# Chunked attention and a mixer on one core: batch 0's values, row sums and first products in another order

## The chip, the cores and the metric

The kernel runs on one core of a Trainium2 chip. TensorE (PE) multiplies matrices, VectorE (DVE), ScalarE (ACT) and GpSimd (POOL) work on elements, SyncE (SP) issues transfers. The metric is the device time of one execution in microseconds (us); less is better.

## What is computed

Four batches, 768 rows, 8 heads of 64 columns. Each chunk of 32 rows attends to the 16 rows before it, itself, the 8 rows behind it and 8 memory rows. What comes out, 512 columns wide, goes through a mixer.

```python
for c in range(S // 32):
    l, r = max(0, 32 * c - 16), min(S, 32 * c + 40)
    k_full = concat([mem_k, k[:, :, l:r]])
    v_full = concat([mem_v, v[:, :, l:r]])
    a = softmax(scale * q_c @ k_full.T)        # the sum gets 1e-9 added
    x[32 * c : 32 * c + 32] = a @ v_full
u = x + ((x.T @ U) @ V).T                      # U is 768 x 32, V is 32 x 768
out = u + relu(u @ w_ch1) @ w_ch2              # 512 x 2048, 2048 x 512
```

U, V and the weights arrive as 64-bit floats; the kernel reads them as pairs of 32-bit words and makes 32-bit numbers from each pair.

## The kernel before

The kernel begins with the attention of batch 0 (`attention(0, xs)`, from L516; its own script stands from L806 to L927). Only when that is done can the mixer of batch 0 (`both_blocks`) and then the other batches (`sevens`) run; their attention is woven into the mixer of the batch before.

Batch 0 goes in three parts of 256 rows (T = 0, 1, 2), each in two sides (s or g = 0, 1) and two tiles of 128 rows (t). A part passes through these steps:

- `load_k`, `load_q` (transfers), `regroup` (L567, copies that sort rows by parity: on VectorE, for part 2 on GpSimd), `k_part` and `q_part` (TensorE turns them, L618; ScalarE and VectorE copy them out of PSUM into `kall` and `qt`).
- `s_turn` (L698): TensorE's scores, 64 small products, 128 records in the trace. `s_weights` (L720, L721, L724): VectorE's maximum and difference, ScalarE's exponential, for each side a tile `pt`. `s_sums` (L729 to L734): VectorE's row sums and their reciprocals `rs`.
- `t_part` (L752): TensorE turns the weights, ScalarE copies them (L755).
- `av_part` (L772): the product with the values in `vbs[T]`, 64 small products; VectorE scales them by `rs` into `x` (L784).
- `collect` (L796): x.T @ U of one tile of 128 rows, into one PSUM bank that holds the sum over all six.

The values come in `load_v` (L600, L607), eight or ten transfers a part, onto a home that GpSimd has filled first with the memory's values, copied to eight blocks of 256 elements (`spread_mv`, L826). U and V are loaded by `load_consts` and made into floats by the class `Words`: `begin` is one ScalarE instruction for each raw tile (L230), then four on VectorE (L237, L245, L250, L257); `u3` is U's result written three times. `spread_v` (L282 to L288) puts V into the form in which it is multiplied. `stream` does the same to the mixer's weights, one step with each `advance(1)`.

When all is collected, `turn_x` (L1133) and `turn_x1` (L1157) turn x for the two blocks of the mixer, and `join_uT` (L1142) adds V's product. `keep_clock(n)` puts n products of a tile of zeros (`busy`, L143) in front of the next bank that TensorE takes.

The order of instructions is written out by hand for SyncE, TensorE, ScalarE, GpSimd and VectorE in this stage (`manual_schedule`): each engine runs its instructions in the order of the script between two `yield`s, with the pieces between `yield`s in order. Each engine waits in order, so an instruction that waits holds all behind it. The small tables at the top (`PROBS`, `GAP`, `LOADS`, `CHAIN`) choose which tiles hold the weights of a part, how many fillers stand where, and the order of the loads.

## Time and profile before

| what | value |
|---|---|
| time, median of 3 runs | 653.67 us (652.35 to 654.86) |
| profiled execution | span 652.5 us from first to last instruction; no time besides is given for it |
| TensorE matmuls busy | 628.0 us, 96% |
| VectorE, ScalarE, GpSimd busy | 367.2, 235.2, 80.9 us |
| attention of batch 0 | about the first 52 us |

A row of a timeline has a start, a duration (both us), the engine, the line, the operation, `out<-in` with shapes, and how often it was merged. In brackets at its end: how long the engine sat idle before it, and what released it. "issue" stands for a wait for nothing that the profile shows. TensorE executes a 32-bit product in two records where the program has one.

### The profile page before, as it was taken

The numbers are of one execution on the slowest core, as the hardware profiler recorded it, in microseconds if no ns is written. First come the engines' busy times: TensorE is split into PE (matmuls) and PEld (weight loads), VectorE is DVE, ScalarE is ACT, GpSimd is POOL, SyncE is SP. The second block draws the span as 40 slices with busy tenths as digits, with TensorE's granted clock in tenths as the row PEclk, the third lists the DMA queues.
The fourth block names the chain that finished last, engine by engine and source line by source line (L and its number), as shares of the span: only waits on it lengthen the run. The fifth ranks groups of instructions, "written<-read, shape, count | busy, mean of one in ns | idle before, by whom it ended". The sixth has DMA issues, their size and how long they took to land.

```text
span 652.5 us, 14945 instructions
## 1 busy us (share of the span) xinstructions
PE 628.0 (96%) x6075; PEld 543.8 (83%) x6078; DVE 367.2 (56%) x703; ACT 235.2 (36%) x557; POOL 80.9 (12%) x106
## 2 busy tenths in 40 slices
PE   8688999999899999999999998999999999999997
PEld 5557899998787888889888897899978899999886
DVE  6947788898784747745643835443445632222322
ACT  4525544447332545522213622321225412121221
POOL 5100000043054465100400000000000000000000
PEclk9989999999999999999999999999999999999999
DMA  9893667667888699676599669667422056555301
GB/s 241 156 354 140 201 221 240 216 204 169 183 183 227 166 314 272 192 187 171 137 258 198 136 178 296 181 179 186 130 70 92 1 172 182 147 162 160 99 2 48
DMA packets 168704, 115.02 MB, mean 176 GB/s; under 512 B 100956, under 2 KB 139484, under 8 KB 168636
## 3 DMA queue, kind: packets, MB, share of 16 engines
q1 hardware_dynamic: 168012, 113.92, 63.0%
q8 instruction: 48, 0.79, 0.5%
q10 hardware_dynamic: 624, 0.15, 0.1%
q14 instruction: 20, 0.16, 0.1%
HBM read 90.83 MB, written 28.97 MB: 184 GB/s over the span
## 4 chain that ended last, share of the span: by engine, by line
PE 61%; DMA 4%; DVE 4%; SPq 2%; issue 1%; ACT 1%; POOL 1%; ACTq 0%
PE ps_h L1301 24%; PE acc L1532 18%; PE acc L1542 9%; DMA blocks<-spread 2%; PE ps_a L772 2%; PE acc L1526 2%; PE ps_h L1481 2%; DMA w1l<-w1s 1%; PE ps_a L698 1%; PE ps_a L1197 1%; SPq L600 1%; PE ps_a L802 1%; PE ps_a L752 1%; DMA w1s<-sums 1%; DVE x L1497 1%
## 5 line engine op out<-in xcount | busy, mean ns | idle before, releaser
L1532 PE MATMUL acc<-w,hh 128*128 128x512 f32 x612 | 158.3, 394 | 0.0
L1532 PEld LDWEIGHTS acc<-w,hh 128*128 128x128 f32 x612 | 112.9, 188 | 19.8 <-issue 0.5
L1542 PE MATMUL acc<-w,hl 128*128 128x512 f32 x306 | 87.2, 393 | 0.0
L1542 PEld LDWEIGHTS acc<-w,hl 128*128 128x128 f32 x306 | 56.8, 188 | 11.9
L1301 PE MATMUL ps_h<-t12h,w1l 128*128 128x384 f32 x192 | 55.8, 344 | 0.6 <-ACT c L1327 0.6
L1301 PE MATMUL ps_h<-bh,w1l 128*128 128x384 f32 x192 | 52.9, 340 | 0.0
L1301 PE MATMUL ps_h<-t34h,w1l 128*128 128x384 f32 x152 | 46.6, 347 | 1.9 <-issue 1.5
L1481 PE MATMUL ps_h<-uh,w1h 128*128 128x384 f32 x124 | 42.5, 347 | 2.2 <-ACT w1h L387 1.2
L1481 PE MATMUL ps_h<-ul,w1h 128*128 128x384 f32 x124 | 41.3, 337 | 0.4 <-DVE ul L1179 0.4
L1316 DVE SCALAR_TENSOR_TENSOR hl<-ps_h,hh 128x384 fp32r<-128x384 f32 x29 | 16.1, 555 | 44.0 <-ACT hh L1315 43.9
L1323 DVE TENSOR_TENSOR c<-ps_h,c 128x384 f32<-128x384 f32 x19 | 10.5, 553 | 51.6 <-PE ps_h L1301 51.6
L1301 PEld LDWEIGHTS ps_h<-t12h,w1l 128*128 128x128 f32 x192 | 35.3, 188 | 3.2 <-ACT c L1327 1.0
L1315 ACT ACTIVATE hh<-hst 128x384 fp32r<-128x384 f32 x36 | 18.9, 526 | 49.9 <-PE acc L1532 44.7
L1316 DVE SCALAR_TENSOR_TENSOR hl<-hst,hh 128x384 fp32r<-128x384 f32 x36 | 20.0, 557 | 29.0 <-PE acc L1542 28.5
L1301 PE MATMUL ps_h<-b,w1l 128*128 128x384 f32 x174 | 35.4, 339 | 0.5 <-DVE hst L1323 0.5
L1301 PEld LDWEIGHTS ps_h<-bh,w1l 128*128 128x128 f32 x192 | 35.1, 188 | 0.8
L1323 DVE TENSOR_TENSOR hst<-ps_h,hst 128x384 f32<-128x384 f32 x36 | 20.0, 555 | 27.4 <-ACT hst L1327 18.0
L1315 ACT ACTIVATE hh<-ps_h 128x384 fp32r<-128x384 f32 x29 | 14.2, 491 | 51.6 <-PE ps_h L1301 51.4
L1301 PE MATMUL ps_h<-t12l,w1l 128*128 128x384 f32 x96 | 32.4, 337 | 0.0
L1301 PEld LDWEIGHTS ps_h<-t34h,w1l 128*128 128x128 f32 x152 | 27.9, 188 | 4.4 <-issue 2.9
L1301 PEld LDWEIGHTS ps_h<-b,w1l 128*128 128x128 f32 x174 | 30.9, 188 | 0.8 <-DVE hst L1323 0.8
L1327 ACT COPY c<-ps_h 128x384 f32<-128x384 f32 x19 | 9.1, 479 | 59.7 <-PE ps_h L1301 59.7
(250 smaller groups left out, 1208.1 us busy)
## 6 DMA issues: line engine op xcount, KB each, us to landing
w1l<-w1s SPq DMA_DIRECT2D x155, 256.0 KB
rw<-in_moe_w_ch_dram SPq DMA_DIRECT2D x14, 512.0 KB
out_dram<-x SPq DMA_DIRECT2D x24, 256.0 KB
blocks<-spread SPq DMA_DIRECT2D x24, 256.0 KB
vb<-in_v_dram SPq DMA_DIRECT2D x56, 98.0 KB
raw<-in_moe_w_ch_dram SPq DMA_DIRECT2D x20, 256.0 KB
rw<-in_moe_w_ch_dram SPq DMA_DIRECT2D x16, 256.0 KB
w1s<-sums SPq DMA_DIRECT2D x16, 256.0 KB
```

Source lines behind the costliest of these rows:

```text
L600: nc.sync.dma_start(out=vt[r0:r0 + NW - NM, n0:n1, D * j:D * j + D], in_=bass.AP(rows.tensor, rows.offset, [[step, count], [CK * step, n1 ...
L698: nc.tensor.matmul(out=psv[s][(slice(CK * i, CK * i + CK), t) + ((p // 2, p % 2) if b >= DIRECT else (p % 2, p // 2))], lhsT=qt[p // 2][ro ...
L772: nc.tensor.matmul(out=psv[g][CK * i:CK * i + CK, t, j], lhsT=pt[s][rows, 2 * t + k_, CK * i:CK * i + CK], rhs=vt[rows, NI * t + i, D * j: ...
L1301: nc.tensor.matmul(out=ps[:, :TOK], lhsT=w_, rhs=u, start=(start and m == 0), stop=(m == 5), skip_group_check=True,)
L1315: nc.scalar.activation(out=hh, in_=c, func=AF.Relu)
L1316: nc.vector.scalar_tensor_tensor(out=hl, in0=c, scalar=0.0, in1=hh.bitcast(F32), op0=ALU.max, op1=ALU.subtract,)
L1323: nc.vector.tensor_tensor(out=out, in0=ps[:, :TOK], in1=in1, op=ALU.add)
L1327: nc.scalar.copy(out=out, in_=ps[:, :TOK])
L1481: nc.tensor.matmul(out=ph[:, :TOK], lhsT=w[:, c, :], rhs=u[c], start=(m == 0), stop=(m + 1 == len(parts)),)
L1526: nc.tensor.matmul(out=acc[tt], lhsT=h[:, sl], rhs=w, start=False, stop=(m == 2))
L1532: nc.tensor.matmul(out=acc[tt], lhsT=h[:, sl], rhs=w, start=(begins and m == 0), stop=False,)
L1542: nc.tensor.matmul(out=acc[tt], lhsT=hl[:, sl], rhs=w2h[f], start=False, stop=ends is not None)
```

## The change

It touches the script of batch 0 alone.

- Loads: memory values, then k and q of part 0, then parts 1 and 2, U, the values of part 0, V, the values of parts 1 and 2, then the weights. V's three transfers thereby go behind the ten of the first values. GpSimd copies the memory's values to the second home right after the first, and to the third right after the memory keys.
- Row sums of parts 0 and 1: `fold` adds halves on GpSimd, six instructions for a side, into the tile `spare`; `invert` adds 1e-9 and takes the reciprocal on VectorE, just before the part's product. Part 2 keeps `s_sums`, behind the product of part 1.
- `t_part(0)` stands before the third scores instead of behind them.
- V's unpacking (`v_words`) stands behind the second weights and before the third ones, on VectorE and ScalarE. U's is one piece sooner.
- `av_part(2)` stands before the collects of tiles 2 and 3, not behind `turn_x`.
- Fillers: three before `av_part(1)`; none before `av_part(2)` and none behind the last collects.
- `PROBS`: the weights of part 1 lie in the tiles 7 and 8 of the second matrix and no longer in 0 and 1.

```diff
-PROBS = [5, 0, 9]
-GAP = [2, 2, 2]
-LOADS = 'mv t1 t2 uv v0 v1 v2 a0 b0 w1 w2'
-CHAIN = [8, 4]
+PROBS = [5, 7, 9]
+GAP = [2, 2, 3]
+LOADS = 'a0 b0 w1 w2'
...
+        def fold(T):
+            rs = rss[T] = sm.tile([P, 2, 2, 2, 2], F32, name="rs", bufs=3)
+            for s in range(2):
+                halves = spare.rearrange("n (s a w) -> n s a w", s=2, w=NW // 2)[:, s]
+                w, wide_ = NW // 2, pts[T, s].rearrange("n (a w) -> n a w", w=NW)
+                while w > 1:
+                    nc.gpsimd.tensor_tensor(
+                        out=halves[:, :, 0:w], in0=wide_[:, :, 0:w], in1=wide_[:, :, w:2 * w], op=ALU.add,
+                    )
+                    w, wide_ = w // 2, halves
+                two_ = halves.rearrange("n (t k g) w -> n t k g w", t=2, k=2)
+                nc.gpsimd.tensor_tensor(
+                    out=rs[:, :, :, :, s].rearrange("n t g k -> n t k g"),
+                    in0=two_[:, :, :, :, 0], in1=two_[:, :, :, :, 1], op=ALU.add,
+                )
+
+        def invert(T):
+            nc.vector.tensor_scalar_add(out=rss[T], in0=rss[T], scalar1=1e-9)
+            nc.vector.reciprocal(out=rss[T], in_=rss[T])
...
             mk = fetch_memk()
-            take(1)
-            take(1)
-            spread_mv(vbs[0])
-            take(2)
+            load(1)
+            load(2)
+            load_U()
+            for n in two:
+                spread_mv(vbs[n])
+                fill_v(n)
+                if n == 0:
+                    load_V()
...
             place_memk()
+            spread_mv(vbs[2])
+            fill_v(2)
+            for what, m in loading:
+                what(m)
             regroup(kraw, kn, "kn", 1)
...
             u_words.begin()
-            s_sums(0)
-            yield
-            keep_clock(GAP[1])
-            sc = s_turn(1)
-            for h in two:
-                q_part(2, h)
             u_words.shift()
             u_words.low()
...
+            yield
+            keep_clock(GAP[1])
+            sc = s_turn(1)
+            fold(0)
             nc.gpsimd.tensor_copy(out=u_sb, in_=u3[:, :, 0, :])
+            for h in two:
+                q_part(2, h)
+            for s in two:
+                t_part(0, s)
             s_weights(1, *sc)
+            v_words.begin()
+            v_words.shift()
+            v_words.low()
+            val = v_words.join()
             yield
             sc = s_turn(2)
-            for s in two:
-                t_part(0, s)
+            fold(1)
             s_weights(2, *sc)
-            v_words.begin()
-            s_sums(1)
+            invert(0)
             av_part(0)
             yield
             for s in two:
                 t_part(1, s)
-            s_sums(2)
-            v_words.shift()
-            v_words.low()
-            val = v_words.join()
+            keep_clock(GAP[2])
+            invert(1)
             av_part(1)
-            take(len(loading))
+            yield
             for s in two:
                 t_part(2, s)
+            s_sums(2)
             for t in two:
                 collect(t)
             spread_v(val)
             yield
             advance(1)
+            wide[0] = None
+            av_part(2)
             for t in two:
                 collect(2 + t)
             early = turn_x(range(NCK))
-            wide[0] = None
-            keep_clock(GAP[2])
             advance(4)
-            av_part(2)
             yield
             advance(1)
             for t in range(4, NT):
                 collect(t)
-            keep_clock(CHAIN[0])
             turned.extend(turn_x1(c) for c in range(3))
```

What that does to the order of instructions, at three places. On GpSimd, from the first copy of the memory's values (`vb_114`, `vb_115` and `vbe` are the homes of parts 0, 1 and 2), before:

```order
L826 COPY vb_114<-mv 128x2048
L626 COPY kall<-memkT 128x32x8 x2
L567 COPY kn<-kraw 128x4x2x64 x2
L826 COPY vb_115<-mv 128x2048
L567 COPY qn<-qraw 128x4x2x64 x2
L826 COPY vbe<-mv 128x2048
L626 COPY kall<-memkT 128x32x8
```

and in the change:

```order
L842 COPY vb_114<-mv 128x2048
L842 COPY vb_115<-mv 128x2048
L627 COPY kall<-memkT 128x32x8 x2
L842 COPY vbe<-mv 128x2048
L568 COPY kn<-kraw 128x4x2x64 x2
L568 COPY qn<-qraw 128x4x2x64 x2
L743 TENSOR_TENSOR spare<-pt 128x256
L743 TENSOR_TENSOR spare<-spare 128x8x16
```

The second and the third copy have gone ahead of the regrouping copies of part 2 (`kn`, `qn`), the second even of the memory keys (`kall`); behind the regrouping the sums of part 0 begin.

On VectorE, from the last instruction of the second weights, before (`mx`, `pt`: weights; `rs`: row sums; `dec` beside `vraw`: V's unpacking):

```order
L721 TENSOR_TENSOR pt<-ps_h,mx 128x512
L710 MEMSET ps_a 32x4x8
L720 TENSOR_REDUCE mx<-ps_a 128x8
L721 TENSOR_TENSOR pt<-ps_a,mx 128x512
L710 MEMSET ps_h 32x4x8
L720 TENSOR_REDUCE mx<-ps_h 128x8
L721 TENSOR_TENSOR pt<-ps_h,mx 128x512
L729 TENSOR_REDUCE rs<-pt 128x2x2x2 x2
L733 TENSOR_SCALAR rs<-rs 128x16
```

and in the change:

```order
L722 TENSOR_TENSOR pt<-ps_h,mx 128x512
L236 TENSOR_SCALAR dec<-dec 96x256
L244 TENSOR_SCALAR dec<-dec 96x256
L249 SCALAR_TENSOR_TENSOR dec<-vraw,dec 96x256
L256 TENSOR_TENSOR dec<-dec 96x256
L711 MEMSET acc_589 32x4x8
L721 TENSOR_REDUCE mx<-acc_589 128x8
L722 TENSOR_TENSOR pt<-acc_589,mx 128x512
L711 MEMSET ps_a 32x4x8
L721 TENSOR_REDUCE mx<-ps_a 128x8
L722 TENSOR_TENSOR pt<-ps_a,mx 128x512
L754 TENSOR_SCALAR rs<-rs 128x16
```

The four instructions of V's unpacking stand before the third weights, and the two sums of part 1 are gone from behind them.

On TensorE, from the first two collects to the turning of x for the second block (`x,uarea`: collects; `dec,rep`: V; `vbe,pt`: third product), before:

```order
L796 MATMUL acc_323<-x,uarea 96x512 x2
L282 MATMUL ps_a<-dec,rep 96x256
...
L796 MATMUL acc_323<-x,uarea 96x512 x2
L1133 MATMUL ps_h<-ident,x 128x128 x6
...
L143 LDWEIGHTS busy
L143 MATMUL ps_a<-busy 128x512
...
L772 MATMUL ps_a<-vbe,pt 32x64 x64
L796 MATMUL acc_323<-x,uarea 96x512 x2
L143 LDWEIGHTS busy
L143 MATMUL ps_a<-busy 128x512
...
L1157 MATMUL ps_a<-ident,x 128x128 x9
```

and in the change:

```order
L817 MATMUL acc_337<-x,uarea 96x512 x2
L283 MATMUL ps_a<-dec,rep 96x256
...
L793 MATMUL ps_a<-vbe,pt 32x64 x64
L817 MATMUL acc_337<-x,uarea 96x512 x2
L1153 MATMUL ps_h<-ident,x 128x128 x6
...
L817 MATMUL acc_337<-x,uarea 96x512 x2
L1177 MATMUL ps_a<-ident,x 128x128 x9
```

The third product has moved ahead of the collects of tiles 2 and 3, and the fillers (`busy`, two before the third product and eight before the last row) are gone.

## Rows read from the trace of the kernel before

**Rows 1.** The page: span, busy us, instruction queue (packets, MB, share).

```profile
span 652.5 us, 14945 instructions
PE 628.0 (96%) x6075; PEld 543.8 (83%) x6078; DVE 367.2 (56%) x703; ACT 235.2 (36%) x557; POOL 80.9 (12%) x106
...
q8 instruction: 48, 0.79, 0.5%
```

**Rows 2.** Stretches: busy us (records) by engine, granted clock, DMA share, GB/s.

```profile
31.00:37.50 6.50, 5.24 (x122) 3.73 (x106) 3.03 (x10) 1.17 (x2) 0.00 (x0) 0.50 0.93 239
...
64.00:100.00 36.00, 36.00 (x184) 32.81 (x183) 30.66 (x53) 15.94 (x35) 0.00 (x0) 1.00 0.66 211
```

**Rows 3.** Timeline of TensorE, where it goes on after a gap in the head.

```profile
28.34 0.30 PE L772 MATMUL ps_h<-vb,pt 64*32 64x64 f32 x2 [0.62 <-ACT pt L755]
...
30.63 0.21 PE L772 MATMUL ps_h<-vb,pt 64*32 64x64 f32 x1 [1.91 <-issue]
...
34.85 1.01 PE L752 MATMUL ps_h<-ident,pt 128*128 128x128 f32 x4 [1.26 <-issue]
```

**Rows 4.** DMA view of 32.4:33.4, 39.4:40.6 and 48.3:49.5: queue, packets, MB, share.

```profile
q8 instruction: 1, 0.02, 5.5%
...
q8 instruction: 1, 0.02, 4.9%
...
q8 instruction: 1, 0.02, 5.1%
```

**Rows 5.** Timeline of GpSimd and VectorE, 4 to 13 us.

```profile
4.93 1.89 POOL L826 COPY vb<-mv 128x2048 f32<-128x2048 f32 x1 [2.40 <-DMA mv<-in_mem_v_dram]
...
5.42 1.68 DVE L567 COPY kn<-kraw 128x512 f32<-128x512 f32 x1 [0.43 <-DMA kraw<-in_k_dram]
7.02 0.75 DVE L567 COPY qn<-qraw 128x512 f32<-128x512 f32 x2
...
9.00 0.46 DVE L314 COPY memkT<-acc 64x64 f32<-64x64 f32 x2 [0.57 <-PE acc L306]
...
11.62 1.17 DVE L567 COPY qn<-qraw 128x512 f32<-128x512 f32 x2
```

**Rows 6.** Timeline of VectorE and GpSimd at U's unpacking.

```profile
18.99 0.26 DVE L237 TENSOR_SCALAR dec<-dec 128x192 int32<-128x192 int32 x1 [0.28 <-ACT dec L230]
19.29 0.46 DVE L245 TENSOR_SCALAR dec<-dec 128x192 int32<-128x192 int32 x1
...
19.23 0.40 POOL L626 COPY kall<-memkT 128x256 f32<-128x256 f32 x1 [1.18 <-PE ps_h L698]
```

**Rows 7.** Groups of GpSimd: names, shapes, count | busy us, mean ns | idle.

```profile
L485 POOL TENSOR_TENSOR vb<-vb 128x256 f32<-128x256 f32 x24 | 18.5, 773 | 1.9
```

**Rows 8.** Timeline of VectorE and ScalarE, 26 to 33 us.

```profile
26.14 0.69 DVE L721 TENSOR_TENSOR pt<-ps_h,mx 128x512 f32<-128x512 f32 x1
...
27.41 0.41 ACT L230 ACTIVATE dec<-vraw 96x256 f32<-96x256 f32 x1
...
31.39 0.23 DVE L237 TENSOR_SCALAR dec<-dec 96x256 int32<-96x256 int32 x1
...
32.43 0.42 DVE L257 TENSOR_TENSOR dec<-dec 96x256 f32<-96x256 f32 x1
```

**Rows 9.** Timeline of TensorE, from the collects to V's product.

```profile
35.65 2.92 PE L796 MATMUL acc<-x,uarea 128*96 128x512 f32 x4
...
44.11 1.48 PE L772 MATMUL ps_a<-vbe,pt 64*32 64x64 f32 x128
46.45 1.96 PE L796 MATMUL acc<-x,uarea 128*96 128x512 f32 x4 [0.86 <-DVE x L784]
48.24 1.89 PE L143 MATMUL ps_a<-busy 128*128 128x512 bf16 x7
49.97 2.17 PE L1157 MATMUL ps_a<-ident,x 128*128 128x128 f32 x18
51.90 0.60 PE L1142 MATMUL ps_h<-v,g 96*128 96x384 f32 x2
```

More of the change, by code (lines that the diff above doesn't have):

```diff
@@ L271, in load_consts, with load_V @@
         )
+    def load_V():
         for g in range(VG):
@@ L809, in attention @@
             for what in LOADS.split():
-                if what == "uv":
-                    loading.append((lambda _: load_consts(), 0))
-                elif what == "mv":
-                    loading.append((lambda _: load_mv(), 0))
-                else:
-                    loading.append(({"t": load, "w": load_w, "a": load_w1, "b": load_w2, "v": lambda T: list(load_v(T))}[what[0]], int(what[1])))
+                loading.append(({"w": load_w, "a": load_w1, "b": load_w2}[what[0]], int(what[1])))
             mv = sm.tile([P, 4 * D], F32, name="mv", bufs=1)
@@ L826, in spread_mv, with fill_v @@
                 nc.gpsimd.tensor_copy(out=home, in_=mv[:, None, :].broadcast_to([P, NB, 4 * D]))
-            def take(n):
-                for _ in range(min(n, len(loading))):
-                    what, m = loading.pop(0)
-                    what(m)
+            def fill_v(T):
+                for _ in load_v(T):
+                    pass
             two = range(2)
-            take(1)
+            load_mv()
             for part in (load_k, load_q):
@@ L838, in attention @@
             mk = fetch_memk()
-            take(1)
-            take(1)
-            spread_mv(vbs[0])
-            take(2)
+            load(1)
[6 more added lines that the diff above has]
+                    load_V()
             keep_clock(START)
@@ L858, in attention @@
             regroup(kraw, kn, "kn", 2)
-            spread_mv(vbs[1])
-            take(1)
             regroup(qraw, qn, "qn", 2)
-            spread_mv(vbs[2])
-            take(2)
             u_words = Words([uraw], nc.vector)
```

2 lines of the change are left out of this document (1 added, 1 removed).

## Prediction

> **What bounds the kernel now.** I read the page first: TensorE matmuls are busy for 628.0 of 652.5 us [rows 1], so the end is set by TensorE, and a change to batch 0 counts only as far as it moves the point from which TensorE is full. The table of stretches says where that point lies: from 64 to 100 us TensorE is busy 36.00 of 36.00 us [rows 2], and little idle time follows. I therefore carry a shift of the head (0 to 52 us) to the end in full; nothing behind it is waiting for a fixed time. The same table shows the granted clock at 0.50, the lower of the two levels, from 31 to 37.5 us, after a gap that ended at 30.63.
>
> TensorE's row of time shows three marks in the head [rows 3]. At 28.34 the second product with values starts, when ScalarE has copied its weights. A few records later it stops, and goes on at 30.63 after 1.91 us with no releaser. At 34.85 the turning of the third weights goes on after 1.26 us with none either, in the midst of four like instructions on one tile. I read these two as waits for TensorE's own instructions. The page's instruction queue moved 48 packets of 0.79 MB in all, 16 KB each, for 6075 and 6078 records, so some 253 records a packet [rows 1]; between the two stops lie about 255. Such a packet runs inside 32.4 to 33.4, before the stop at 34.85 ends, the next only inside 39.4 to 40.6, and the one after inside 48.3 to 49.5 [rows 4]. So a block seems to be asked for when the one before it is entered, and came 4.2 us later (30.63 to 34.85); the next one started 4.6 us after 34.85, and with the same 1.5 us from a packet's end to TensorE's going on it was usable some 7.1 us after. Counting on, the block after that was entered at about 44.95, in the third product, and was usable about 6.0 us later. The transfers of weights were then under way. All of these are estimates from those rows.
>
> **The second copy of the memory values goes ahead on GpSimd.** A copy of 2048 elements takes GpSimd 1.89 us [rows 5]. VectorE's regrouping copy that fell into it took 1.68 us, where its like takes 0.4 (two in 0.75 us), and ended 0.28 us after GpSimd's [rows 5]. In the change the next such copy follows at once, so VectorE's qn copies, which stand at 7.02, wait about 1.9 us more. Of that the 0.57 us that VectorE waits at 9.00 [rows 5] is slack; the third such copy now meets the later regrouping copies and costs some 0.5 (two of them lost 0.42 in this way at 11.62, 1.17 for 0.75 [rows 5]). I take +1.8 us at the first scores and all behind them. Bounds: 0, if the copies slip in between; 3.7, if two are met in full.
>
> **The values' loads.** They go ahead of V by three DMA issues. No wait of TensorE in rows 3 is for them, and the first product waits for ScalarE, so 0. V arrives later by ten issues, but ScalarE takes it up only behind the second exponentials, which I expect later still, so 0 again; its bound is the few us of those issues.
>
> **The sums of parts 0 and 1 leave VectorE.** Part 0's stand right before the unpacking of U, which waited for ScalarE at 18.99 [rows 6]; taking them out only lengthens that idle time: 0. Part 1's and the later place of part 2's stand behind the third weights: 0 for TensorE. What they add counts: 24 GpSimd instructions, six a side, the first on 256 elements at 0.77 us [rows 7] and each next on half as many; with a fixed part of 0.2 that is some 2.3 us a side, an estimate. Part 0's stand beside VectorE's five instructions on U, part 1's beside the four on V. Rows 6 show the price: the second instruction on U took 0.46 us, where the first took 0.26, because a GpSimd copy of 0.40 ran from 19.23. I let each of the nine wait for one GpSimd instruction, 0.3 us on average: +1.5 on U and +1.2 on V. Bounds: 0 and 0.77 each. The Trainium skill (SBUF — State Buffer, SBUF: two separate sides) has the pair of ports held for a whole instruction also against a VectorE instruction with two inputs in SBUF; rows 6 show it for one with a single input alone. If only those were held, +0.6 and +0.5 would stand for these two figures.
>
> **V's unpacking moves ahead of the third weights.** VectorE's four instructions took 1.46 us, from 31.39 to 32.85 [rows 8]; there they cost TensorE nothing, here they stand before work it needs. They also wait for ScalarE: after VectorE's last second weights come an exponential (0.6) and the unpacking of V (0.41 [rows 8]), so 1.1 us of idle VectorE. With the 1.2 above: +3.8. The third weights, done at 26.83 [rows 8], are done 1.8 + 1.5 + 3.8 = 7.1 us later, near 33.9.
>
> **First weights turned ahead of the third scores; ScalarE.** TensorE's turning of part 0 is earlier, and the wait of the first product goes. But ScalarE's copies of the turned second weights stand behind both third exponentials, as they did, and V's unpacking (0.3 to the next instruction) no longer stands between, so they come 6.8 us later, and the second product could start at 28.34 + 6.8 = 35.1 [rows 3]. Before it was stopped until 30.63, so the path gains only +4.5. The three fillers ahead of it run in a wait.
>
> **The next block of code.** It was usable 4.2 us after its predecessor's entry at 30.63, and 7.1 after the entry at 34.85. The entry at 35.1 is nearest to the second; but the load then depends on how far the weights' transfers are, so I take half of the difference: +1.4, bounds 0 and 2.9.
>
> **The end of the head.** From 34.85 to the first product of V at 51.90 are 17.05 us [rows 9]. Out of it go the eight fillers, 48.24 to 49.97 (1.73), the two before the third product at the same rate (0.4), and the wait of the last collects (0.86) [rows 9]: what the fillers bridged, the eviction of the collects, is as well bridged by the 1.93 us of turning behind them. That is -3.0. Late in the third product, some 5.5 us after the entry (0.8 of turning, 2.9 of collects, 0.6 for V by the row at 51.90, and 1.25 of the product's 1.48 [rows 9]), the next block begins, which is usable 6.0 to 7.1 us after the entry: +0.5, by the nearer entry at 44.95; bounds 0 and 1.6.
>
> **Sum.** 4.5 + 1.4 - 3.0 + 0.5 = +3.4 us: 655.9 against the profiled execution's span of 652.5. No other time of that execution is given; the median is 653.67, 1.17 above the span, so I forecast **657.1**, slower. Its own range is 655.4 to 659.4. Half a per cent, which a measurement of this kernel can just tell from no change, is 3.3 us, so slower begins at 656.94.
>
> **Rivals.** (1) *The waits between VectorE and GpSimd stay off the path.* If copies and sums slip in between each other, the third weights are late by 1.46 + 1.1 = 2.5 us alone, ScalarE's copies are there by 30.5, before the code stop ends, and -3.0 + 0.5 is left: 651.2. With the early 1.8 us but no others it is 653.0. For it: at 11.62 two copies lost 0.42 us and not the whole of a GpSimd copy each [rows 5], so short instructions hurt less than long ones. Against it: the 1.68 us at 5.42 [rows 5]. It decides if the second product starts before 30.7. (2) *Code is not late.* If the block asked for at 35.1 comes as fast as at 30.63 and the last one in time, it is 4.5 - 3.0 = +1.5: 655.2. If the old stop of 1.26 us at 34.85 goes too, it is 653.9. For it: TensorE now waits for data before 35.1, which gives a block time to come; against it: the 4.6 us before the packet inside 39.4 to 40.6 began [rows 4]. The Trainium skill (Runtime: NRT & Kernel Launch, Instruction fetch mechanics) says that the cost of entering a block is mostly hidden; that gives the 653.9, and rows 3 speak against it. (3) *The clock.* TensorE idles longer in the change (28 to 35 us), and a second stop in the third product could keep or put the clock at the lower level through the following collects and turning. The stretch from 31 to 37.5 [rows 2] is what one such fall did; 6.5 us of work at half rate would add about 3.3: 660.5.
>
> **How the numbers follow.** Forecast 0.48, rival 1 0.20, rival 2 0.22, rival 3 0.10. Slower by over 0.5%: most of the forecast and rival 3, 0.48. Within: the rest of the forecast, rival 2 and the larger part of rival 1, 0.44. Faster: 0.08, the part of rival 1 in which the early code stops shrink too. The range reaches from 651.0 (rival 1 with nothing late) to 661.2 (rival 3, and the upper bounds of the code terms).
>
> **What would show it.** Right: a VectorE regrouping copy of over 1.5 us near 7 to 9 us; instructions on U and V twice as long as before; the third exponentials ending near 34; the second product starting near 35 for ScalarE's copies; a code stop near 40; no fillers behind the last collects; the first product of V near 55. Wrong: a second product that starts before 31, or a V product before 51.

## The result, and the profile after

The change is slower: 662.47 us, median of 4 runs (661.28 to 665.31), against 653.01 (652.08 to 654.86) for the kernel before beside it; ratio 1.0146, 95% interval 1.0114 to 1.0177. A second set gave 661.46, ratio 1.0122 (1.0089 to 1.0156). The forecast of 657.1, 3.4 us above the time before, had the sign right and about a third of the size, and 662.47 lies above its range (651.0 to 661.2). The profiled execution took 663.17 us with a span of 661.4: 8.9 more than the span before [rows 1].

The page of the change, and its stretches (length, busy us and records of PE, PEld, DVE, ACT, POOL, granted clock, DMA share, GB/s):

```profile
span 661.4 us, 14957 instructions
PE 629.0 (95%) x6071; PEld 544.9 (82%) x6071; DVE 370.8 (56%) x699; ACT 235.1 (36%) x557; POOL 89.9 (14%) x130
```
```profile
29.50:32.50 3.00, 3.00 (x76) 2.56 (x62) 2.86 (x7) 0.86 (x2) 0.98 (x4) 0.50 0.62 139
39.70:46.30 6.60, 5.80 (x17) 2.69 (x16) 0.00 (x0) 1.17 (x2) 0.00 (x0) 0.50 1.06 396
210.50:213.50 3.00, 3.00 (x10) 2.52 (x9) 1.99 (x6) 0.49 (x1) 1.35 (x2) 0.50 0.22 43
```

TensorE is busy 1.0 us longer than before (629.0 for 628.0), though it has seven fillers fewer: more of its work ran at the lower clock. The other 7.9 us of the 8.9 are idle time. Three stretches show 0.50, where rows 2 had one. TensorE's timeline, at the places that answer to rows 3 and rows 9 (and further down the place where the second batch's product with values stops):

```profile
28.81 0.21 PE L793 MATMUL ps_a<-vb,pt 64*32 64x64 f32 x1 [2.35 <-issue]
...
33.43 0.30 PE L793 MATMUL ps_h<-vb,pt 64*32 64x64 f32 x2 [0.15 <-ACT pt L776]
...
40.50 0.80 PE L773 MATMUL ps_a<-ident,pt 128*128 128x128 f32 x3 [4.92 <-issue]
...
41.95 3.62 PE L817 MATMUL acc<-x,uarea 128*96 128x512 f32 x4
...
47.53 1.47 PE L793 MATMUL ps_a<-vbe,pt 64*32 64x64 f32 x126 [0.68 <-DVE v L289]
...
48.92 1.96 PE L817 MATMUL acc<-x,uarea 128*96 128x512 f32 x4
...
55.11 2.17 PE L1177 MATMUL ps_a<-ident,x 128*128 128x128 f32 x18
...
57.04 0.59 PE L1162 MATMUL ps_h<-v,g 96*128 96x384 f32 x2
...
194.20 1.84 PE L1552 MATMUL acc<-w2last,hh 128*128 128x512 f32 x6 [0.57 <-DVE x L1517]
...
209.44 0.34 PE L793 MATMUL ps_a<-vb,pT 64*32 64x64 f32 x14 [3.50 <-issue]
```

The first scores start at 13.77 (11.43 before, +2.3). The third turning goes on at 40.50 (34.85, +5.65). V's first product comes at 57.04 (51.90, +5.14), and the product at 194.20 stood before at 188.78: +5.42, so the loss of the head (all up to V's first product) is carried. Then a stop of 3.50 us comes that the trace before does not have, with a stretch at half rate behind it (3.4 us, so some 1.7 lost); a stop of 1.46 us at 408 in the trace before is gone. 5.42 + 3.50 + 1.7 - 1.46 = 9.2, beside the 8.9 of the spans. This compares one execution of each kernel.

VectorE and GpSimd in the first 13 us, the answer to rows 5:

```profile
5.25 1.53 DVE L568 COPY kn<-kraw 128x512 f32<-128x512 f32 x1 [0.60 <-DMA kraw<-in_k_dram]
6.70 2.45 DVE L568 COPY qn<-qraw 128x512 f32<-128x512 f32 x2
...
10.04 2.60 DVE L568 COPY kn<-kraw 128x512 f32<-128x512 f32 x2
```
```profile
4.61 3.92 POOL L842 COPY vb<-mv 128x2048 f32<-128x2048 f32 x2 [2.06 <-DMA mv<-in_mem_v_dram]
...
10.27 2.09 POOL L842 COPY vbe<-mv 128x2048 f32<-128x2048 f32 x1
```

Two copies took 2.45 us where the same two took 0.75 [rows 5], and two more 2.60 beside the third GpSimd copy.

### The profile page after: what moved, and what is told of

It reads as the page before. It is cut to its first block, busy times and chain, and to the rows that moved or that the text cites. A ratio compares the mean times of both kernels' runs of the same rounds, so it can differ in the third digit from the quotient of the medians.

```text
span 661.4 us, 14957 instructions
## 1 busy us (share of the span) xinstructions
PE 629.0 (95%) x6071; PEld 544.9 (82%) x6071; DVE 370.8 (56%) x699; ACT 235.1 (36%) x557; POOL 89.9 (14%) x130
## 4 chain that ended last, share of the span: by engine, by line
PE 58%; DMA 4%; DVE 4%; SPq 2%; issue 2%; POOL 1%; ACT 1%; DVEq 0%; POOLq 0%; ACTq 0%
PE ps_h L1321 23%; PE acc L1552 18%; PE acc L1562 9%; PE ps_a L793 2%; PE ps_h L1501 2%; PE acc L1546 2%; DMA blocks<-spread 1%; DMA w1l<-w1s 1%; PE ps_a L1217 1%; PE ps_a L699 1%; PE ps_a L823 1%; PE ps_a L773 1%; POOL vb L486 1%; DMA vb<-mv 1%; DMA w1s<-vb 1%
## 5 line engine op out<-in xcount | busy, mean ns | idle before, releaser
L1321 PEld LDWEIGHTS ps_h<-bh,w1l 128*128 128x128 f32 x192 | 35.1, 188 | 0.8
L1335 ACT ACTIVATE hh<-ps_h 128x384 fp32r<-128x384 f32 x29 | 14.2, 490 | 52.0 <-PE ps_h L1321 52.0
L1509 ACT ACTIVATE hh<-ps_h 128x384 fp32r<-128x384 f32 x31 | 15.2, 492 | 43.0 <-PE ps_h L1501 43.0
```

What stands on the lines that cost most here:

```text
L1321: nc.tensor.matmul(out=ps[:, :TOK], lhsT=w_, rhs=u, start=(start and m == 0), stop=(m == 5), skip_group_check=True,)
L1335: nc.scalar.activation(out=hh, in_=c, func=AF.Relu)
L1509: nc.scalar.activation(out=hh, in_=ph[:, :TOK], func=AF.Relu)
```

## The experiments

All ratios are to the kernel before, run beside each. Two theories were put against each other: **data** (the forecast's: waits of VectorE, ScalarE and GpSimd set the head) and **code** (TensorE's blocks of 256 instructions set it, each asked for when the one before is entered, and late when transfers are under way). A block is one packet of 16 KB of the instruction queue [rows 1]; it is entered when its first instruction runs; a stop is idle time of TensorE that the profile puts down to "issue".

**The change once more.** No edit.

> The change itself once more, for a time beside the others on the same chip and for a second trace. Theory A (the length of TensorE's stops for code is set by what the transfers' queues hold when a block is asked for, so it differs from execution to execution): the stops stand at the same instructions as in the first trace, but their lengths differ by up to 3 us; the time is 658 to 664, the median 661 to 662. Theory B (the stops belong to the order of the program): the same lengths within 0.3 us, at 28.81, 40.50 and 209.44.

661.46 us, ratio 1.0122 (1.0089 to 1.0156). TensorE's longest waits in this second trace, and a row of ScalarE ahead of the last one:

```profile
31.75 0.21 PE L793 MATMUL ps_a<-vb,pt 64*32 64x64 f32 x1 [4.01 <-issue]
...
42.56 0.49 PE L773 MATMUL ps_a<-ident,pt 128*128 128x128 f32 x3 [4.55 <-issue]
...
57.91 0.59 PE L1162 MATMUL ps_h<-v,g 96*128 96x384 f32 x2
...
207.27 0.34 PE L793 MATMUL ps_a<-vb,pT 64*32 64x64 f32 x14 [0.73 <-issue]
...
270.25 0.66 PE L773 MATMUL ps_a<-ident,pt 128*128 128x128 f32 x4 [2.97 <-ACT pt L725]
```
```profile
266.56 0.41 ACT L489 CAST vb<-vb 128x256 fp32r<-128x256 f32 x1 [1.46 <-DMA w1s<-vb]
```

Same places, other lengths: 4.01 for 2.35, 4.55 for 4.92, 0.73 for 3.50. Counted from the start of the trace, with TensorE's waits for semaphores, the three stops stand in both traces at instructions 961, 1473 and 4801, that is 2 and 13 times 256 apart: at ends of blocks. The wait at 270.25 is not of this kind: it stands at instruction 5664, within a block, and was for ScalarE's exponential (`pt`); ScalarE and VectorE had waited for a transfer just before (row at 266.56). In the head the two traces agree within 1 us at V's product; the rest of the program differs by 1.9 us (604.4 and 602.4 from V's product to the end).

**Every block's end moved by 64 products.** Eight fillers at the start became 72 thin products.

```diff
-            keep_clock(START)
+            keep_clock(START - 8)
+            keep_place(72)     # 64x32 by 64x64 products of zeros
```

> The change with eight of the twelve fillers at the start replaced by 72 thin products (64x32 by 64x64), which end in the wait for the first k, so that every block of TensorE's instructions ends 64 products sooner in the program, and nothing else moves. Theory A (the stops of 2.35 us at 28.81 and of 4.92 us at 40.50 are blocks that are asked for when the block before is entered, and come 1.2 to 5.1 us later, so they depend on where the ends lie): the block that is entered in the first product with values is asked for near 25 to 27 us, the next one in the middle of the second product; the stop in the first turning of the third weights goes or moves by more than 2 us, some stop of 1 to 5 us may stand at another place behind 34 us; the head's end (57.0) moves by 2 us or more, either way, 658 to 664. Theory B (these two waits are for data or for the clock): both stops stay at the same instructions, and the time stays within 0.7 of the change.

662.12 us, ratio 1.0106 (1.0074 to 1.0138). The stop in the third turning is gone, and others stand where blocks now end:

```profile
18.37 0.24 PE L707 MATMUL ps_a<-kall,qt 64*32 64x64 f32 x1 [2.81 <-issue]
...
24.94 0.21 PE L707 MATMUL ps_a<-kall,qt 64*32 64x64 f32 x1 [1.15 <-issue]
...
33.48 0.21 PE L801 MATMUL ps_a<-vb,pt 64*32 64x64 f32 x1 [2.43 <-issue]
...
39.33 0.31 PE L801 MATMUL acc<-vb,pt 64*32 64x64 f32 x1 [0.56 <-issue]
...
55.33 0.60 PE L1171 MATMUL ps_h<-v,g 96*128 96x384 f32 x2
```

So the stops without a releaser belong to the ends of blocks, not to data: no data moved. V's product came 1.7 to 2.6 us sooner, but the time is that of the change: what the head gained was not kept behind it.

**Weights late.** Nine loads of weights are issued by ScalarE behind its copies of the third weights.

```diff
-            for what, m in loading:        # behind the third values, on SyncE
-                what(m)
...
             for s in two:
                 t_part(2, s)
+            for what, m in loading:        # on ScalarE's queue
+                what(m)
```

> The change with the first nine loads of weights issued by ScalarE behind its copies of the turned third weights, in the place of SyncE's at 30.5 us. Theory A (a block asked for waits behind the weights' transfers: 4.25 us from the entry at 33.81 to the packet at 38.06, where 1.1 to 1.6 us is usual in the head without them): the packet comes within 2 us of the entry, the stop in the first turning of the third weights shrinks from 4.92 to 1.5 to 2.5 us, the granted clock does not fall at 40 us, and the head's end comes 3 to 5 us sooner if the weights are not missed; 657 to 660. Rival (the fetch is slow by itself): the stop stays over 4 us and the time over 661, more with the weights late.

659.61 us, ratio 1.0100 (1.0072 to 1.0129). Two transfer views show what the late weights altered: in the change, the 4.1 us from the entry of the block in the second product to the next block's packet (33.8 to 37.9); here, 2.6 us from such an entry on (34.4 to 37; queue: packets, MB, share):

```profile
q1 hardware_dynamic: 708, 1.08, 92.2%
```
```profile
q8 instruction: 1, 0.02, 2.6%
...
q1 hardware_dynamic: 6, 0.01, 0.6%
```

The first has no packet of instructions at all; in the second it is there, and the other transfers' queue stands almost idle. TensorE then shows:

```profile
37.97 0.49 PE L775 MATMUL ps_a<-ident,pt 128*128 128x128 f32 x3 [1.91 <-issue]
...
45.44 0.86 PE L795 MATMUL ps_a<-vbe,pt 64*32 64x64 f32 x41 [4.00 <-DVE v L289]
...
56.97 0.60 PE L1166 MATMUL ps_h<-v,g 96*128 96x384 f32 x2
```

The stop fell from 4.92 (4.55 in the second trace) to 1.91 us, as the code theory had it. But ScalarE's nine issues now stood ahead of its casts of V, and the third product waited 4.00 us for them, so V's product came no sooner. That wait is my edit's, and the time can't be told from the change's (the intervals overlap).

**GpSimd's copies back.** The second and third copies, and the loads onto them, behind the regrouping of part 2's k and q. SyncE issues the weights behind those loads, as in the change.

```diff
-            for n in two:
-                spread_mv(vbs[n])
-                fill_v(n)
...
+            spread_mv(vbs[0])
+            fill_v(0)
...
-            spread_mv(vbs[2])
-            fill_v(2)
-            for what, m in loading:
-                what(m)
...
             regroup(kraw, kn, "kn", 2)
+            spread_mv(vbs[1])
+            fill_v(1)
             regroup(qraw, qn, "qn", 2)
+            spread_mv(vbs[2])
+            fill_v(2)
+            for what, m in loading:
+                what(m)
```

> The change with GpSimd's second and third copies of the memory values, and the loads onto them, where the kernel before has them (behind the regrouping of part 2's k and of its q). Theory of the prediction (VectorE's regrouping waits for GpSimd's copies): the first scores start 1.8 to 2.3 us sooner (11.5 for 13.77), the regrouping copies of part 1 take 0.4 us again; but as the block of code is asked for at entry, the end moves by less: 660.5 to 662. Rival (these waits are for the transfers, whose order and traffic changed too): the first scores stay within 0.5 us.

657.96 us, ratio 1.0050 (1.0017 to 1.0084): the largest gain of a single edit. VectorE, then TensorE:

```profile
6.92 0.75 DVE L568 COPY qn<-qraw 128x512 f32<-128x512 f32 x2
...
9.09 0.89 DVE L568 COPY kn<-kraw 128x512 f32<-128x512 f32 x2
```
```profile
27.98 0.26 PE L793 MATMUL ps_a<-vb,pt 64*32 64x64 f32 x1 [3.72 <-issue]
...
36.27 0.49 PE L773 MATMUL ps_a<-ident,pt 128*128 128x128 f32 x3 [2.43 <-issue]
...
43.67 0.41 PE L793 MATMUL ps_a<-vbe,pt 64*32 64x64 f32 x18 [1.94 <-issue]
...
53.79 0.59 PE L1162 MATMUL ps_h<-v,g 96*128 96x384 f32 x2
```

The copies are short again and the first scores start at 11.16 (13.77 and 14.64 in the two traces of the change). V's product gained 3.3 to 4.1 us beside these, some 0.6 more than the first scores did, and the time more than I expected. But the edit moved transfers too. The first issue of the weights by SyncE's queue, in the change and here, and the instruction queue here from 32.1 to 34.9:

```profile
30.49 1.27 SPq L335 DMA_DIRECT2D rw<-in_moe_w_ch_dram  x1
```
```profile
33.05 0.45 SPq L335 DMA_DIRECT2D rw<-in_moe_w_ch_dram  x1
```
```profile
q8 instruction: 1, 0.02, 2.9%
```

In the change the weights were issued 3.3 us before the block in the second product was entered (33.81); here the entry, at 32.11, came 0.9 us before them, and the next block's packet 1.45 us after it, not 4.25. The stop in the third turning was 2.43 us, not 4.92 or 4.55. So this edit undoes a part of the late code as well, and how much of its gain the copies alone are worth is not shown.

**The weights' loads back.** In the kernel before, all but the first two loads of weights stand behind the second product, onto the tiles that part 1's weights leave; the change freed them of that (`PROBS`).

```diff
-PROBS = [5, 7, 9]
+PROBS = [5, 0, 9]
...
-            for what, m in loading:
-                what(m)
+            what, m = loading.pop(0)       # the first two
+            what(m)
...
             av_part(1)
+            for what, m in loading:        # all but the first two, on SyncE
+                what(m)
```

> The change with the loads of weights after the first two behind the second product again, and part 1's weights in tiles 0 and 1, as before; SyncE issues them. Theory A (weights under way make the code late): from the entry in the second product to the packet 1 to 2 us (4.25 in the change), the stop in the third turning 1.5 to 2.5 us (4.92, 4.55), no lower clock at 40 us, V's product 2 to 3 us sooner; time 658 to 660. Rival (the code stops are as long under the values' transfers): the stop stays over 4 us, 661 to 662.5.

658.39 us, ratio 1.0069 (1.0035 to 1.0102). TensorE:

```profile
30.53 0.21 PE L793 MATMUL ps_a<-vb,pt 64*32 64x64 f32 x1 [3.98 <-issue]
...
38.91 0.49 PE L773 MATMUL ps_a<-ident,pt 128*128 128x128 f32 x3 [2.16 <-issue]
...
46.80 0.41 PE L793 MATMUL ps_a<-vbe,pt 64*32 64x64 f32 x18 [2.42 <-issue]
...
55.25 0.60 PE L1164 MATMUL ps_h<-v,g 96*128 96x384 f32 x2
```

The stop in the third turning is half as long, the next block is late instead, and V's product gains 1.8 to 2.7 (in an execution of 662.02 us, above this run's median). The ratio's interval is clear of that of the change's first set, not of the second's. It is a part of the diff that the forecast gave no price of its own.

**V's words back** behind the third weights.

```diff
             s_weights(1, *sc)
-            v_words.begin()
-            v_words.shift()
-            v_words.low()
-            val = v_words.join()
...
             s_weights(2, *sc)
+            v_words.begin()
...
```

> The change with V's unpacking on VectorE and ScalarE behind the third weights again. The prediction gave its place +3.8 us at the third weights. Theory of the prediction: the third weights end 2.5 to 3.8 us sooner (near 29.5 for 32.9), the second product starts sooner by as much, and the time falls by 2 to 3: 659 to 660. Theory A (code sets the pace: TensorE can't enter the next block less than 3.7 to 4.0 us after the one before): the third weights end sooner, but the stop at 28.81 and the blocks behind it stay, and what the second product gains (at most 1.5 us, as it can't start before the first is done and turned) is lost again in the next stop: 661 to 662.

662.40 us, ratio 1.0136 (1.0089 to 1.0183), V's product at 57.54: no gain that can be told, as the code theory had it. ScalarE's row of the last third weights and TensorE's stops:

```profile
30.54 0.63 ACT L725 ACTIVATE pt<-pt 128x512 f32<-128x512 f32 x1 [0.92 <-DVE pt L722]
```
```profile
31.61 0.26 PE L793 MATMUL ps_a<-vb,pt 64*32 64x64 f32 x1 [4.00 <-issue]
...
41.71 0.80 PE L773 MATMUL ps_a<-ident,pt 128*128 128x128 f32 x3 [4.38 <-issue]
```

The third weights were ready at 31.17, before the first product had even gone on; the wait of 3.8 us that the forecast put on the path was beside a wait for code.

**Row sums back on VectorE, and the turning back.** First the sums in the place of the reciprocals; then `t_part(0)` behind the third scores (each alone).

```diff
-            fold(0)
...
-            invert(0)
+            s_sums(0)              # likewise for part 1
```

> The change with the row sums of parts 0 and 1 on VectorE as before, each in the place where the change takes the reciprocals; no fold on GpSimd. In the change the third block of the head's instructions is entered 6.6 to 7.1 us after the second (18.30 to 24.87, 19.14 to 26.19), as the third scores wait for the second weights; the kernel before took 3.65. Theory of the prediction (the folds hold VectorE's instructions on U up): the second weights come 1.0 to 1.5 us sooner, the third block is entered some 5.3 us after the second, and the first V product comes 1 to 1.5 us sooner: time 660 to 661. Rival (VectorE waits for ScalarE's copies and U itself, not for GpSimd): no difference there, 661.5 to 662.5.

```diff
-            for s in two:
-                t_part(0, s)
             s_weights(1, *sc)
...
             sc = s_turn(2)
+            for s in two:
+                t_part(0, s)
```

> The change with the turning of the first weights behind the third scores again; nothing else. Theory A (the third scores take their two PSUM banks before the turning again, so they no longer wait for VectorE's second differences, and the blocks behind are asked for sooner): the wait of 1.6 us in the third scores goes, the third block is entered 4 to 5 us after the second in the place of 6.6 to 7.1, the 2.4 to 4.0 us stop in the first product turns into a wait for ScalarE's copies or goes, and V's product comes 2 to 4 us sooner: 657.5 to 660. Rival (VectorE's second and third weights set the pace, whatever the order on TensorE): V's product stays within 1 us of 57.0 to 58.0 and the time at 661 to 662.5.

660.51 us (1.0101; 1.0068 to 1.0134) and 661.13 us (1.0098; 1.0063 to 1.0133). Both intervals overlap those of the change, so each may be worth nothing; from the ends of the intervals a few us can't be ruled out. With the turning back, the third scores no longer waited, but the first product waited 2.05 us for ScalarE's copies instead and the third turning still 4.48 for code.

**Several parts back.** Copies and sums; the same with the weights issued by ScalarE behind V's casts; copies, sums and turning; copies and weights' loads; and all of these with V's words (left: the order of the first loads, U's words, the tail, three fillers).

> The change with both undone: GpSimd's copies of the memory values in their old places, the row sums on VectorE. If the two are independent their gains add: 4.4 us of the copies' place and what the sums gave alone (0 to 1.5): 656 to 658 beside 662 of the change. If both only feed the same stops for code, the sum gives no more than the copies alone: 658.

> As the run with copies and sums undone, and the first nine loads of weights issued by ScalarE behind V's three casts, so that no bulk transfer runs while the blocks of the third turning and of the third product are fetched. Theory A (a fetch waits behind the weights' transfers): the packets behind the second product's block and the next come 1.0 to 2.0 us after the entry, not 4, the stop in the third turning is under 2 us, and V's product comes 1.5 to 3 us sooner than without; if the weights are not missed, 653.5 to 656. Rival (late weights are missed by what stands behind the head): the gain in the head is lost between 57 and 75 us, 657 to 660.

> As e13, with the copies of the memory values in their old places and the row sums on VectorE too. What is left of the change is the order of the loads, the earlier place of the words of U and V, the tail and the fillers. If e13's part and the copies' part add: 656.8 (the run with the two undone) - 2 to 4 = 653 to 655. If nothing but these three was harmful, it should reach the kernel before with the new tail, 650 to 652. Rival: no gain over the run with the two undone, 656 to 657.5.

> The change with GpSimd's copies of the memory values and the loads of weights in their old places. If these two are the change's harm, their gains add: 4.4 + 2 to 3 us, 654.5 to 656.5 beside some 653.5 of the kernel before. If the weights' place gives nothing: 658.

> The change with copies, sums, turning, V's words and the weights' loads all in their old places; left are the order of the first loads (parts 1 and 2 of k and q, U and the first values ahead of V), U's words one piece sooner, the new tail and three fillers ahead of the second product. If the five parts are the whole harm it is the kernel before with the new tail: 650 to 652, ratio 0.994 to 0.997. If the order of the first loads or U's words cost something: 653 and more.

| undone | median us | ratio (95%) |
|---|---|---|
| copies, sums | 656.78 | 1.0065 (1.0040 to 1.0090) |
| copies, sums, weights late | 655.39 | 1.0021 (0.9990 to 1.0052) |
| copies, sums, turning | 657.70 | 1.0069 (1.0045 to 1.0092) |
| copies, weights' loads | 657.87 | 1.0045 (1.0016 to 1.0075) |
| copies, sums, turning, V's words, weights' loads | 653.93 | 0.9989 (0.9961 to 1.0016) |

The gains do not seem to add. Against the first ratio (1.0146), copies and weights' loads gave back 0.96 and 0.77 percentage points alone, and 1.01 together; the intervals leave this open, but the traces agree with it. Both edits shorten the same stop, to 2.43 and 2.16 us alone and, together, to this:

```profile
36.25 0.49 PE L773 MATMUL ps_a<-ident,pt 128*128 128x128 f32 x3 [2.63 <-issue]
```

The sums and the turning give nothing that can be told beside the copies. Late weights, now free of V's casts, bring the ratio from 1.0065 to 1.0021, with intervals that still overlap. With copies, sums and late weights the loss is no longer clear of zero, and with everything back neither; whether the whole gain of the tail (below) is then left, these intervals don't say.

**The tail alone**, on the kernel before; then the same with late weights.

```diff
-            for t in two:
-                collect(2 + t)
-            early = turn_x(range(NCK))
             wide[0] = None
-            keep_clock(GAP[2])
-            advance(4)
             av_part(2)
+            for t in two:
+                collect(2 + t)
+            early = turn_x(range(NCK))
+            advance(4)
...
-            keep_clock(CHAIN[0])
```

> The kernel before with the change's last part alone: the last product with values ahead of the collects of tiles 2 and 3, no fillers ahead of it and none behind the last collects. The prediction gave this -3.0 us. In the change the product then waited 0.67 us for VectorE's part of V and its break before that was 0.3, so I now expect -2.0 in the head (V's product near 50 for 51.9). Ten products fewer also move the blocks' ends, whose stops behind the head differ by 3 us from execution to execution: 650 to 653. Rival (the tail gives nothing, since the waits replace the fillers): 653 to 654.

> The kernel before with the new tail, and all loads of weights but the first two issued by ScalarE behind V's casts. Theory A (fetches wait behind the weights' transfers in any order of the program): as in the run with copies and sums undone, where late weights gave 1.4 us at the median (656.78 to 655.39), 1 to 2 us less than with the new tail alone: ratio to the kernel before 0.991 to 0.994 in the place of 0.9944. Rival (this head asks for its blocks before the weights anyway, and the weights are missed behind it): 0.995 or more.

**650.56 us, ratio 0.9944 (0.9909 to 0.9980)**: this one part of the change, put on the kernel before, beats both kernels. With late weights besides, 652.68 us, 0.9972 (0.9945 to 0.9998): no more. The trace of the latter, the fastest of its 12 executions, shows what the head can be when no stop is long:

```profile
33.94 0.60 PE L754 MATMUL ps_h<-ident,pt 128*128 128x128 f32 x4 [2.13 <-issue]
...
37.76 1.64 PE L774 MATMUL ps_a<-vbe,pt 64*32 64x64 f32 x126 [0.67 <-DVE v L288]
...
47.44 0.60 PE L1144 MATMUL ps_h<-v,g 96*128 96x384 f32 x2
```
```profile
core 0: 646.0 us, clock 1.000
```

V's product is 4.5 us sooner than before [rows 9], and the granted clock was 1.000 throughout. From the third turning to V's product it is 13.50 us, where the kernel before took 17.05.

**Three that settled little.** The stop at 209: the change with seven thin products behind its last collects, so that it has as many products as before; and the kernel before with seven fillers fewer there. And one block more in the kernel before.

```diff
+            keep_place(7)              # change, behind the last collects
```
```diff
-CHAIN = [8, 4]
+CHAIN = [1, 4]                         # kernel before
```
```diff
+            keep_place(128)            # kernel before, ahead of the second product
```

> The change with seven thin products of zeros (64x32 by 64x64) behind the last collects, where the eight fillers stood, so that TensorE has as many products up to there as the kernel before. Theory A (what lies behind the head depends on where TensorE's 16 KB blocks of instructions end, and the change moved these ends by seven products): the stop of 3.50 us at 209 us in the change and the lower clock for 3.4 us behind it go, and the 1.45 us stop that the kernel before has at 408 us comes back; span 661.4 - 3.5 - 1.7 + 1.3 = about 657.5, time about 658.6. Theory B (the stop at 209 us comes from the phase of the transfers against TensorE, not from the place of the block): it stays, and the time is that of the change, 662.5 within 0.7.

> The kernel before with one filler behind the last collects in the place of eight; nothing else. Its own cost: 7 x 0.216 = 1.5 us less at most, if what follows is ready then (the row at 51.90 allows 0.6 for the wait behind them). Theory A (place of the block ends): a stop of about 3.5 us appears in the product with values of the second batch, some 5.4 us sooner than in the change (near 204 us), and the one at 408 us goes: 653.0 - 1.5 + 3.5 + 1.7 - 1.4 = 655.3. Theory B: no stop there, and the time is 651.5 to 652.5.

> The kernel before with 128 thin products of zeros (64x32 by 64x64, 256 records, one block of 16 KB) ahead of the second product with values. As work they are 128 x 0.015 = 1.9 us, and part of it falls into the stop of 1.91 us that stands there. Theory A (a block of code takes 3.7 to 4.2 us from entry to entry, whatever it holds): the head gets 3.7 to 5 us longer, 657 to 659. Theory B (the work counts, not the code): at most 1.9 us, 653 to 656.

With seven back: 661.10 us, ratio 1.0104 (1.0050 to 1.0158), and a stop of 1.21 us at that place. The kernel before with seven fewer: 654.15, 1.0004 (0.9979 to 1.0029), with this row:

```profile
200.12 0.34 PE L772 MATMUL ps_a<-vb,pT 64*32 64x64 f32 x14 [3.25 <-issue]
```

So seven fillers fewer went with the stop in this trace, and the time they save was given back. But the change's second trace has 0.73 us there, at the same ends of blocks: the place allows the stop, its length is not set by the place. One block more cost 0.93% (0.64 to 1.21), but its thin products took 49 ns each and not 15 (121 records in 5.96 us), so the work alone would explain it, and V's product came only 1.8 us later (53.69): no verdict.

## Why the prediction was wrong

Two steps failed: that nothing behind the head is waiting for a fixed time, and the price of the end of the head. The account in us, beside the first trace:

| stretch | forecast | measured |
|---|---|---|
| up to the third turning | 4.5 + 1.4 = +5.9 | +5.65 |
| from there to V's product | -3.0 + 0.5 = -2.5 | -0.5 |
| behind the head | 0 | +3.8 |
| all | +3.4 | +8.9 |

With either of the two put right, this execution would have stayed within the range (658.7 or 660.5 us under 661.2).

**Head carried in full: right for the head, wrong for the rest.** +5.14 at V's product is +5.42 at 194 us. But the step said that nothing behind waits on a moment of its own. The blocks of code do: 3.50 + 1.7 - 1.46 = +3.7 us came behind the head. In the second trace it was 7.8 (span 660.3) less 6.0 (V's product) = 1.8, with a stop for code of 0.73 and the wait of 2.97 for data at 270. How much of this belongs to the change is not settled: from V's product to the end the kernel before took 600.6 in its one trace, but 604.1 with seven fillers fewer, and all traces together range from 598.6 to 606.6.

**Copies ahead, +1.8: right in kind, small.** The first two copies met cost 1.7, near the 1.9 forecast (2.45 for 0.75). The third GpSimd copy was to cost 0.5; it cost 1.85 (2.60 for 0.75), and the first scores came 2.3 later. Undone, the place of the copies gave back 0.7 to 1.0% (ratio 1.0050 for 1.0122 and 1.0146), but that edit also issued the weights later, as shown above.

**Sums, +1.5 on U and +1.2 on V: mis-sized on U.** VectorE's five instructions on U took 20.80 to 23.00, 2.20 us, for 1.95 before: +0.25. The second weights left VectorE 2.06 us later than before (25.73 for 23.67), no more than the first scores had come late, so on the path the sums beside U cost nothing. The four on V took 2.33 for 1.46: +0.87.

**V's words, +3.8: the size was right, the path was not.** They and their wait took 3.43 us, from the last second difference (25.73) to VectorE's next work (29.16), and the third weights left VectorE at 32.24, not 33.9 (ScalarE at 32.90). Undoing it gave nothing that the runs can tell. Here the step failed that the second product waits for ScalarE alone: in the change the first product stops for code before it, and with V's words back that stop, 4.00 us, still stood before it.

**Second product and the next block: right in sum, by two errors.** The third turning was to come at 34.85 + 4.5 + 1.4 = 40.75; it came at 40.50. But the product started at 33.43, not 35.1, and the next block took 6.7 us from the entry at 33.81, where 5.6 was allowed and up to 7.1 within the bounds. Rival 1 (second product before 30.7) and rival 2 (code not late) are both refuted. The Trainium skill (Runtime: NRT & Kernel Launch, Instruction fetch mechanics) has the cost of entering a block mostly hidden; 2.35 and 4.92 us in one head are not.

**The tail, -3.0 + 0.5: failed in the change.** It came out at 16.54 us for 17.05, -0.5. The fillers and the wait of 0.86 did go. But the third product stood right behind V's spreading and waited 0.68 us for VectorE's part of V (row at 47.53), which the sum put at nothing. And the lower clock that followed the stop at 40.50 lasted to about 46.3, where before it ended near 37.5 [rows 2]: some 3 us more at half rate, or 1.5 lost (an estimate). The first four collects took 3.62 us for 2.92 [rows 9]; four at the upper level take 1.96. In the trace with tail and late weights, where the clock held, the stretch was 3.55 us shorter. So the saving is there, and what took most of it in the change is the clock, which this sum had left out.

**Rival 3 as a rival.** It priced a fall of the clock at +3.3 and shared out chances between it and the code forecast as if only one could hold. Both held: each fall in the first trace began within 1 us of the end of a stop for code (28.81, 40.50, 209.44). The clock's mean over each run tells it for all eight runs of the change: 0.983 to 0.992 (median 0.988), where 102 of 114 runs of the kernel before have 0.995 or more (median 0.997). At 0.988, 2 x 0.012 x 660 = 15.8 us run at the lower level, against 4 at 0.997; the difference is at most 6 us of work, an estimate, as TensorE is idle in some of it.

**The range.** The forecast's own range, 655.4 to 659.4, does not come out of its bounds: 4.5 - 3.0 = 1.5 and 4.5 + 2.9 - 3.0 + 1.6 = 6.0 give 655.2 to 659.7. Neither would have held the result.

What stays open: why two stops at the same block ends differ by 3 us from execution to execution; what sums and turning are worth; what the copies' place is worth without the later weights; how much of the loss behind the head belongs to the change; and whether all parts undone (0.9989) and the tail alone (0.9944) differ at all, as their intervals overlap: if they do, the order of the first loads or U's words may hold it.

## What to carry to other kernels

Where an engine runs hundreds of very short instructions, count its blocks of code first: here 256 records are done in 1.5 us (row at 44.11 [rows 9], 128 products with their weight loads), and between the blocks of the head that TensorE stood waiting for lay 3.65 us at the least (17.38 to 21.03 in the trace before). So a wait for data that is removed can come back as a wait for code. Keep bulk loads out of such a stretch, and look at what a freed buffer lets start early. And price the rivals together when one brings on the other: stops for code, the fall of the clock behind them, and more stops later in the program.

## What the hardware showed that I had not expected

- In the head a block's packet came after the block before it had been entered, and not further ahead (in the change: entries at 28.81, 33.81 and 40.50, packets at 29.96, 38.05 and 45.59). From the entry to the packet it took about 1 to 3.3 us until the weights were under way (3.95 once, with the ends of blocks moved), and mostly 3.4 to 5.6 with the weights under way; from the packet's end to TensorE's going on, 1.2 to 1.7 us where TensorE stood waiting (38.05 + 0.88 to 40.50, for one).
- The granted clock fell beside the stops of 2.35, 4.92 and 3.50 us in the change's first trace, and beside one of 1.91 us in the trace before [rows 2, rows 3]. It did not fall beside the 2.13 us stop of the fastest trace, nor behind the wait of 2.97 us at 270 in the change's second trace (1.00 from 270.5 to 274). So the length of one stop does not tell.
- GpSimd's instructions with two inputs cost VectorE's five on U little (0.25 us in all) and the four on V 0.87, while GpSimd's large copies held VectorE's plain copies for nearly their whole length (1.70 us more beside copies of some 1.96, half of 3.92). The Trainium skill (SBUF — State Buffer, SBUF: two separate sides) names, of VectorE's instructions, copies between places in SBUF and those with two inputs there as the ones that contend with GpSimd. The first agrees with the 2.45 us; an instruction of the second kind lost 0.11 us at most on U here (0.47 for 0.36), and 0.57 on V (0.99 for 0.42).
- Executions of one and the same kernel differ by 5 us (651.84 to 657.15 in 24 runs of the kernel before). The stops differ by up to 3 us at one place; that they make up that difference is not shown.
